# Seventeen late prefetch slots in the room of the split activations, four experts' second weights by column halves, a second result buffer and outputs in four pieces

## The chip, the cores and the metric

The kernel runs on one core of one Trainium2 chip. Times are device microseconds of that core: the median of the runs of one kernel, and for the profile the time of one profiled execution and its span from the first to the last instruction.

## What is computed

Three layers follow one another. Pooled softmax attention over 32 heads gives x (2304 tokens by 512). A feed-forward layer with an ELU replaces it. Last comes a soft mixture of eight experts: a softmax over the tokens gives each of 32 slots a weighted sum of tokens, each expert runs its four slots through two matrices, and a softmax over the slots spreads the results back over the tokens.

```
scores = scale * np.matmul(q_pool, k.transpose(0, 1, 3, 2))     # per head, 576 x 1152
attn_out = softmax(scores) @ v
h = x @ w_in;  g = np.where(h > 0.0, h, np.exp(np.minimum(h, 0.0)) - 1.0);  x = g @ w_out
logits = x @ phi                                                # 2304 x 32
slot_input = softmax(logits, 0).T @ x
for e in range(E):
    slot_out[e] = np.maximum(slot_input[e] @ w1[e], 0.0) @ w2[e]
return softmax(logits, 1) @ slot_out
```

`w1` is (8, 512, 1024) and `w2` is (8, 1024, 512), both float32: 33.5 MB together, read once. The output is 2304 x 512 float32, 4.7 MB.

## The kernel before

The whole program is first recorded as a list of operations (`add`), each with a due time, a duration, what it reads and what it writes. `Plan.run` then lays them out on the five engines by a list schedule, and the order that it finds is the order in which each engine's instructions are emitted. Space in the on-chip memory is carved by name out of a few big tiles: `memr` (split operands of TensorE), `memf` (plain float32), `memy` and `memz`. `plan.region` tells the planner which names share space, so an operation on a name waits for all users of the names that held the space before it. `swap` closes the big tiles `memy` and `memz` late in the program and opens new ones in their room, called `memyq` and `memzq`. Every DMA that the sections below speak of is issued from SyncE (SP), in order.

In the attention and feed-forward phases TensorE works on operands split into a high and a low part. The parts of the ELU's result are `H#` and `L#`, five buffers each, in `memr`. `C3T` holds the final softmax (`combine`, one call for each of the four batches, with five transposes each at L1105), `xn1` to `xn3` and `XN` the token tiles of the last slot sums (`tok_all`, L1038 to L1048).

The last phase streams the expert weights. They are cut into 64 units of 512 KB each. Units 0 to 31 are `w1` (rows of 4 KB), used by `stage1` (L1230). The others are `w2`, used by `stage2` (L1266): 24 units of kind 2 (whole rows, 2 KB) for the first six experts, and for the last `NLAST` = 2 experts eight units of kind 3, which hold one half of the columns (rows of 1 KB), first all of half m = 0, then all of half m = 1. `spare` lists the slots that hold a unit: 18 in `memyq` and `memf`, which come free during the feed-forward phase, and 11 in `memzq`, which come free when the feed-forward phase has ended. A unit whose number is past the slots goes into the slot of an earlier one, in a ring, once TensorE has read that; two of the slots are used only once. When half m is complete in `psC`, `finish(m)` (L1279 to L1304) sums it, multiplies by `C3T`, scales nine pairs of token tiles on VectorE and ScalarE into one buffer `OSB`, and writes them in pieces of `OGRP` = 6 tiles, so six output DMAs of 768 KB in all. Both halves use the same `OSB`.

Of the kernel before, what the change touches and what calls it, by code (L numbers as in the profile page):

```python
# [26 lines left out]
def act(n, psum=False):  # L27
    return n * 0.0009 + (0.135 if psum else 0.165)
# [6 lines left out]
def dve2(n):  # L35
    return n / 1920 + 0.145
# [14 lines left out]
class Plan:  # L51
# [11 lines left out]
    def add(self, t, eng, dur, fn, r=(), w=(), size=0.0, mode="F", port=False, fixed=False):  # L63
        if isinstance(eng, str):
            eng, dur = (eng,), (dur,)
        cls = (self.tag or str(self.phase)) + "".join(x.rstrip("0123456789") for x in w[0][:2] if isinstance(x, str)) + (eng[0] if len(eng) == 1 else "*")
        self.ops.append([t, len(self.ops), eng, dur, fn, r, w, size * (0.75 if self.phase == 2 else 1.0), BIAS[3 if self.tag else self.phase], t + PRI.get(cls, 0.0), cls, mode, port, fixed])

    def region(self, name, lo, hi):
        self.base[name] = (lo, hi)  # L70
# [196 lines left out]
EP = 1.3  # L267
SLOT = 14.8061
EAV = [26.8636, 30.7913, 35.1115]
OGRP = 6  # L270
DQ = [-10, 0.61]
DK = [[-9, 0.3], [-9, 0.3]]
UC = -14
# [6 lines left out]
TOKLAG = 2.0  # L280
TAIL0 = 21.9927
CMB = 2.7419
NLAST = 2


@with_exitstack
def attention_moe_softmoe(
# [12 lines left out]
    nc = tc.nc  # L300
# [207 lines left out]
    def copy_(out_, in_):  # L508
        return lambda e: nc.scalar.copy(out_, in_) if e == "ACT" else nc.vector.tensor_copy(out_, in_)  # L509
# [346 lines left out]
    def elu(n, f, t):  # L856
        A, uk, ek, hk, lk = (("A", "h", n, f), ("E", "m", n, f), ("U", "m", n, f), ("H", "m", n, f), ("L", "m", n, f))

        def ph():
            return got(psA, A)[:, :, :NH]  # L860

        add(t, "ACT", act(NQ, True), lambda: nc.scalar.activation(got(Ef, uk), ph(), AF.Relu, scale=-1.0), r=[A], w=[uk])  # L862
        add(t + 0.6, "ACT", act(NQ), lambda: nc.scalar.activation(
            got(Uf, ek), got(Ef, uk), AF.Exp, scale=-1.0), r=[uk], w=[ek])
        add(t + 1.2, "DVE", dve(NQ), lambda: nc.vector.scalar_tensor_tensor(
            got(Ef, uk), got(Uf, ek), -1.0, ph(), ALU.add, ALU.max), r=[ek, A], w=[uk])
        add(t + 2, ("ACT", "DVE"), (act(NQ), dve2(NQ)), lambda e: copy_(got(Hr, hk), got(Ef, uk))(e), r=[uk], w=[hk])
        add(t + 2.6, ("DVE", "Pool"), (dve(NQ), pool(NQ)),
            lambda e: sub_(got(Lr, lk), got(Ef, uk), r32(got(Hr, hk)))(e), r=[uk, hk], w=[lk] + ([("elu", f)] if n == NSLOT - 1 else []))

    def o_mm(n, c, t, t0):
        w, b = slots[n]
        g = w % NG
        last = n == NSLOT - 1
        x = KD * t + c
        k = x % 2 if last else t
        po_, ck = (lambda: psC[k][:, :NH]), ("C", k)
        if last and x % 4 > 1:
            ck = ("A", "o", c, t)
            po_ = lambda: got(psA, ck)[:, 0, :NH]  # L880
        d = X[b][:, c, t * NH : (t + 1) * NH]

        def mm():
            i = 0
            for f in range(GF):
                o = f * DM + c * P
                h, l = got(Hr, ("H", "m", n, f))[:, t], got(Lr, ("L", "m", n, f))[:, t]
                wh, wl = (BW["o", w % 2, x]()[:, o : o + P] for x in "hl")
                for a, x in ((wh, h), (wh, l), (wl, h)):
                    nc.tensor.matmul(po_(), lhsT=a, rhs=x, start=(i == 0), stop=(i == 3 * GF - 1))  # L890
                    i += 1
# [26 lines left out]
    def logits_split(b, t0):  # L918
        A = ("A", "lg", b)
        for c in range(KD):  # L920
            hk, lk = ("H", "lg", b, c), ("L", "lg", b, c)
            src = v3(X[b][:, c], 2)
            xr = [("X", b, c, 0), ("X", b, c, 1)]

            def mm(c=c, hk=hk, lk=lk):
                for x in (got(Hr, hk), got(Lr, lk)):
                    for t in range(2):
                        nc.tensor.matmul(got(psA, A)[: 2 * NS, t, :NH], lhsT=PH[:, c], rhs=x[:, t],
                                         start=(c == 0 and x is got(Hr, hk)), stop=(c == KD - 1 and x is got(Lr, lk)))
# [341 lines left out]
    def finish(m, t):  # L1271
# [12 lines left out]
        for x in range(0, NT, per):  # L1284
# [90 lines left out]
```

## Time and profile before

| | us |
|---|---|
| median of 3 runs | 997.66 |
| lowest and highest of the 3 | 996.82, 1002.28 |
| the profiled execution's own time | 997.68 |
| its span, first to last instruction | 995.6 |

TensorE is busy for 958.6 us of the span. The profile's page cuts the span into 40 slices of 24.9 us. The feed-forward phase ends near 905 us. What follows is the last 90 us: slot sums, expert weights and outputs.

### The profile page before, as it was taken

What the parts mean: (1) busy time and instruction counts of PE and PEld (TensorE: products, weight loads), DVE (VectorE), ACT (ScalarE), POOL (GpSimd) and SP (SyncE); (2) the same over time, 40 slices, a digit from 0 to 9 for tenths busy, and PEclk for the clock granted to TensorE, in tenths of its full rate; (3) what the DMA queues carried; (4) which work ended last, traced back from release to release, by engine and by line L of the source; (5) the groups of instructions that cost most, each with busy time, mean ns of one, the idle gap of its engine ahead of it and who ended that gap; (6) DMA issues with size and microseconds to landing.
All of it is one profiled execution on the core that took longest, in us unless ns stands there. A gap on an engine that the chain in (4) does not pass through costs nothing.

```text
span 995.6 us, 20896 instructions
## 1 busy us (share of the span) xinstructions
PE 958.6 (96%) x8474; PEld 783.5 (79%) x8474; DVE 760.4 (76%) x1281; ACT 496.9 (50%) x887; POOL 396.3 (40%) x278
## 2 busy tenths in 40 slices
PE   7999999999999999999999999999999999998965
PEld 5777767766777777766899999999999999996423
DVE  6677798888888787899998989989758887765103
ACT  2555566555666566566664444443434475442102
POOL 2878888798888888897200000000000000000000
PEclk7999999999999999999999999999999999998996
DMA  7133424223334342202362332334330132315797
GB/s 175 45 86 85 106 73 122 72 78 113 85 85 116 85 105 61 88 16 67 105 201 89 104 121 95 107 99 162 139 116 28 43 127 86 123 47 230 288 377 267
DMA packets 101583, 114.86 MB, mean 115 GB/s; under 512 B 43632, under 2 KB 70768, under 8 KB 101488
## 3 DMA queue, kind: packets, MB, share of 16 engines
q1 hardware_dynamic: 101488, 113.55, 37.3%
q8 instruction: 66, 1.08, 0.4%
q14 instruction: 29, 0.24, 0.1%
HBM read 100.27 MB, written 13.18 MB: 114 GB/s over the span
## 4 chain that ended last, share of the span: by engine, by line
PE 85%; DVE 8%; DMA 4%; ACT 1%; SPq 1%; issue 1%; DVEq 0%; ACTq 0%
PE psC L890 20%; PE psA L851 20%; PE psC L690 14%; PE psA L683 10%; PE psS L683 5%; PE psA L614 3%; PE psS L614 3%; DVE memf L623 2%; DMA memf<-in_moe_w_dram 2%; PE psC L714 1%; PE psA L598 1%; PE psA L1230 1%; DMA memzq<-in_moe_w_dram 1%; PE psA L575 1%; DVE memf L557 1%; PE psC L659 1%
## 5 line engine op out<-in xcount | busy, mean ns | idle before, releaser
L704 POOL TENSOR_TENSOR memf<-memf 128x576 f32<-128x576 f32 x241 | 360.1, 1496 | 61.4 <-ACT memf L695 35.2
L890 PE MATMUL psC<-memr,memz 128*128 128x288 f32 x1512 | 224.7, 297 | 1.2 <-DVE memf L901 0.7
L890 PEld LDWEIGHTS psC<-memr,memz 128*128 128x128 f32 x1512 | 208.1, 188 | 4.4 <-ACT memf L509 1.6
L690 PE MATMUL psC<-memf 128*64 128x288 f32 x1152 | 174.2, 419 | 0.0
L695 ACT ACTIVATE memf<-psA 128x576 f32<-128x576 f32 x206 | 132.8, 651 | 63.0 <-PE psA L614 54.8
L623 DVE TENSOR_REDUCE memf<-psA 128x2 f32<-128x384 f32 (+3 forms) x235 | 142.5, 618 | 27.6 <-PE psA L614 14.1
L1335 POOL MEMSET memf<- 128x2048 f32 x1 | 1.8, 1809 | 388.4 <-DVE memr L512 388.4
L901 DVE TENSOR_TENSOR memf<-psC,memf 128x288 f32<-128x288 f32 x220 | 100.3, 463 | 47.6 <-PE psC L890 46.0
L623 DVE TENSOR_REDUCE memf<-psS 128x4 f32<-128x768 f32 (+1 forms) x140 | 103.5, 740 | 38.3 <-PE psS L614 20.5
L690 PEld LDWEIGHTS psC<-memf 128*64 128x64 f32 x1152 | 69.8, 136 | 48.6 <-issue 9.3
L851 PE MATMUL psA<-memz 128*128 128x288 f32 x512 | 93.8, 295 | 0.0
L862 ACT ACTIVATE memf<-psA 128x576 f32<-128x576 f32 x64 | 41.8, 652 | 102.8 <-PE psA L851 102.8
L509 ACT CAST memr<-memf 128x576 fp32r<-128x576 f32 x72 | 48.2, 674 | 74.4 <-PE psC L890 35.9
L851 PEld LDWEIGHTS psA<-memz 128*128 128x128 f32 x512 | 76.6, 188 | 0.0
L683 PE MATMUL psA<-memr 64*128 64x288 f32 x816 | 72.1, 299 | 1.8 <-DVE memf L623 1.8
L695 ACT ACTIVATE memf<-psS 128x576 f32<-128x576 f32 x82 | 53.4, 651 | 40.9 <-PE psS L614 35.4
L512 DVE TENSOR_TENSOR memr<-memf,memr 128x576 fp32r<-128x576 f32 x80 | 62.8, 791 | 6.4 <-ACT memr L509 5.9
L683 PEld LDWEIGHTS psA<-memr 64*128 64x128 f32 x816 | 59.1, 185 | 8.6 <-issue 3.9
L683 PE MATMUL psA<-memy 64*128 64x288 f32 x624 | 61.5, 302 | 0.0
L851 PE MATMUL psA<-memz,memv 128*128 128x288 f32 x256 | 52.0, 296 | 0.0
L683 PEld LDWEIGHTS psA<-memy 64*128 64x128 f32 x624 | 47.7, 188 | 4.1 <-issue 3.5
L509 ACT COPY memf<-psC 128x288 f32<-128x288 f32 (+1 forms) x66 | 26.2, 397 | 49.3 <-PE psC L1266 26.7
(209 smaller groups left out, 1602.5 us busy)
## 6 DMA issues: line engine op xcount, KB each, us to landing
memf<-wscr SPq DMA_DIRECT2D x32, 512.0 KB
memf<-in_moe_w_dram SPq DMA_DIRECT2D x30, 512.0 KB
memzq<-in_moe_w_dram SPq DMA_DIRECT2D x22, 512.0 KB
memz<-in_q_dram SPq DMA_DIRECT2D x32, 288.0 KB
memz<-in_k_dram SPq DMA_DIRECT2D x32, 288.0 KB
memf<-in_v_dram SPq DMA_DIRECT2D x16, 576.0 KB
memf<-in_moe_w_in_dram SPq DMA_DIRECT2D x32, 256.0 KB
wscr<-memf SPq DMA_DIRECT2D x32, 256.0 KB
```

The source lines that it names most:

```text
L509: return lambda e: nc.scalar.copy(out_, in_) if e == "ACT" else nc.vector.tensor_copy(out_, in_)
L512: return lambda e: ENG[e].tensor_tensor(out_, a, b, ALU.subtract)
L614: nc.tensor.matmul(tile_[:m, j, lo : lo + n * MW], lhsT=qkb["qh", i][js, o : o + m], rhs=qkb["kh", i][js, g * MW : (g + n) * MW], start=Tr ...
L623: add(t, "DVE", dve(2 * n * MW), lambda: nc.vector.reduce_max(MX[i][:m, a, :, g : g + n], v4(got(psS, tok)[:m, :, lo : lo + n * MW], n), a ...
L683: nc.tensor.matmul(sp[:, j, :NH], lhsT=qkb[w, i][js, cs] if w else ONER[js], rhs=qkb[m, i][js, hs], start=(x == 0), stop=(x == 3))
L690: nc.tensor.matmul(psC[h][j * D : (j + 1) * D, :NH], lhsT=VR[i][:, j, c], rhs=e[:, j], start=(c == 0), stop=(c == NC - 1))
L695: add(t + 0.01, "ACT", act(NQ, True), lambda: nc.scalar.activation(got(EAf, E_), got(psS, S_)[:, :, :NH], AF.Exp, scale=1.0 / 16.0), r=[S_ ...
L704: ENG[e].tensor_tensor(ac, a, got(EAf, E_), ALU.add)
L851: nc.tensor.matmul(ph[:, t, :NH], lhsT=a, rhs=x, start=(i == 0), stop=(i == 3 * KD - 1))
L862: add(t, "ACT", act(NQ, True), lambda: nc.scalar.activation(got(Ef, uk), ph(), AF.Relu, scale=-1.0), r=[A], w=[uk])
L890: nc.tensor.matmul(po_(), lhsT=a, rhs=x, start=(i == 0), stop=(i == 3 * GF - 1))
L901: add(t0 + 0.8, "DVE", dve(NH), lambda: nc.vector.tensor_tensor(d, po_(), d, ALU.add), r=[ck], w=XK)
```

## The change

- `H#` and `L#` move from `memr` to the end of `memz`, which grows by their room (5,760 floats in each partition); `memr` shrinks by as much. When `memz` is swapped for `memzq`, its room holds 17 slots instead of 11, so there are 35 slots in place of 29.
- `xn1` to `xn3`, which used the room of `H#`, now lie over `C3T` and `C3`, and `SO3` over `XN`.
- `NLAST` is 4: the last four experts' `w2` goes by column halves, 16 units of kind 3 and 16 of kind 2.
- Half m = 1 has a result buffer of its own, `OS1`, in `memzq`.
- Each half is written in four pieces: 2, 4, 6 and 6 tiles for m = 0, and 6, 6, 4 and 2 for m = 1.
- The planner counts a weight's transfer at 0.67 of its size in place of 0.75.

```diff
-OGRP = 6
+OGRP = [[2, 6, 12, 18], [6, 12, 16, 18]]
-NLAST = 2
+NLAST = 4
...
-    SIZE = {"r": 15232 - 2 * KD * NQ, "f": 24456, "v": ND, "y": KD * NQ * 2, "z": 7 * ND + 2 * KD * NQ}
+    SIZE = {"r": 15232 - 2 * KD * NQ - 10 * NQ, "f": 24456, "v": ND, "y": KD * NQ * 2, "z": 7 * ND + 2 * KD * NQ + 10 * NQ}
...
-    Hr = [v3(x, 2) for x in carve("r", "H#", 5, NQ)]
-    Lr = [v3(x, 2) for x in carve("r", "L#", 5, NQ)]
+    zo = 7 * ND + 2 * KD * NQ
+    Hr = carve("z", "H#", 5, NQ, off=zo, late=True)
+    Lr = carve("z", "L#", 5, NQ, off=zo + 5 * NQ, late=True)
...
-        kind, off = ("v", 0) if i == 0 else ("r", plan.base[("H#", 0)][0] - BASE["r"] + (i - 1) * 2 * DM)
+        kind, off = ("v", 0) if i == 0 else ("r", plan.base[("C3T", 0)][0] - BASE["r"] + (i - 1) * 2 * DM)
...
-    SO3 = over("r", "SO3", 2, HM, "H#", 0, 4 * ND)
-    OSB = v3(over("f", "OSB", 1, NT * HM, "X", 2)[0], NT)
+    SO3 = over("r", "SO3", 2, HM, "XN")
+    OS0 = v3(over("f", "OS0", 1, NT * HM, "X", 2)[0], NT)
+    oz = 12 * ND
+    plan.region(("OS1", 0), BASE["z"] + oz, BASE["z"] + oz + NT * HM)
...
-    spare("z", 0, ts(32.55), 11)
+    spare("z", 0, ts(32.55), 17)
...
-            if (x + per) % OGRP == 0:
-                t0 = x + per - OGRP
-                dma(t + 2.7 + 0.3 * (x + per), out[t0 * P : (x + per) * P, m * HM : (m + 1) * HM].rearrange("(a p) c -> p a c", p=P),
-                    OSB[:, t0 : x + per], [("OSB", 0, y) for y in range(t0, x + per, per)] + [("loads", 0)], [("out", m, t0)], 512 * OGRP * HM, 0.5)
+            if x + per in OGRP[m]:
+                t0 = max([0] + [y for y in OGRP[m] if y <= x])
+                add(t + 2.7 + 0.3 * (x + per), "SP", 0.5, lambda t0=t0, t1=x + per: nc.sync.dma_start(
+                    out[t0 * P : t1 * P, m * HM : (m + 1) * HM].rearrange("(a p) c -> p a c", p=P), osb(m)[:, t0:t1]),
+                    r=[(f"OS{m}", 0, y) for y in range(t0, x + per, per)] + [("loads", 0)], w=[("out", m, t0)], size=512 * (x + per - t0) * HM)
```

Up to the last feed-forward slot the order of every engine is the same in both programs. The rows that follow are SyncE's DMAs, from the last units loaded ahead of `memzq` to the end; `in_moe_w_dram` is either expert matrix, and the last column is the tile (128x1024 is a `w1` unit, 128x2x512 a unit of kind 2, 128x4x256 one of kind 3). Before:

```order
L1215 DMA memf<-in_moe_w_dram 128x1024 x3
L515 DMA memf<-wscr 128x1024
L1215 DMA memf<-in_moe_w_dram 128x1024 x3
L1215 DMA memzq<-in_moe_w_dram 128x1024 x11
L1215 DMA memyq<-in_moe_w_dram 128x1024 x3
L1215 DMA memyq<-in_moe_w_dram 128x2x512
L1215 DMA memf<-in_moe_w_dram 128x2x512 x12
L1215 DMA memzq<-in_moe_w_dram 128x2x512 x11
L1215 DMA memyq<-in_moe_w_dram 128x4x256 x4
L1215 DMA memf<-in_moe_w_dram 128x4x256 x4
L515 DMA out_dram<-memf 128x6x256 x6
```

And of the change, from the same place:

```order
L1226 DMA memf<-in_moe_w_dram 128x1024
L1226 DMA memf<-in_moe_w_dram 128x2x512 x2
L520 DMA memf<-wscr 128x1024
L1226 DMA memf<-in_moe_w_dram 128x1024 x3
L1226 DMA memzq<-in_moe_w_dram 128x1024 x16
L1226 DMA memzq<-in_moe_w_dram 128x2x512
L1226 DMA memyq<-in_moe_w_dram 128x2x512 x4
L1226 DMA memf<-in_moe_w_dram 128x2x512 x9
L1226 DMA memf<-in_moe_w_dram 128x4x256 x3
L1226 DMA memzq<-in_moe_w_dram 128x4x256 x13
L1322 DMA out_dram<-memf 128x2x256
L1322 DMA out_dram<-memf 128x4x256
```

Behind these stand two pieces of six tiles from `memf` and four pieces of 6, 6, 4 and 2 tiles from `memzq`. From the first `memzq` row on there are 46 units in both programs: 14 of `w1`, 24 of kind 2 and 8 of kind 3 before, and 16, 14 and 16 now; 17 of them wait only for `memzq`, where 11 did.

The next rows are TensorE's between the last slot sums (L1042, L1047 now) and the first matmuls of `stage1` (L1230, L1241 now). L1105 (L1110 now) are `combine`'s transposes, L1322 (L1334 now) turns the finished slot sums. Before:

```order
L1042 MATMUL psC_80<-memr 64x512 x6
L1105 MATMUL psB_6063<-ident,memr 96x128
L1105 MATMUL psB_6064<-ident,memr 96x128
L1105 MATMUL psB_6063<-ident,memr 96x128
L1105 MATMUL psB_6064<-ident,memr 96x128
L1322 MATMUL psB_6063<-slot_sum,memf 128x32 x4
L1105 MATMUL psB_6064<-ident,memr 96x128 x2
L1105 MATMUL psB_6063<-ident,memr 96x128
L1230 MATMUL psA_78<-memyq,memf 32x512 x4
```

And of the change:

```order
L1047 MATMUL psC_80<-memr 64x512 x6
L1334 MATMUL psB_6064<-slot_sum,memf 128x32 x4
L1110 MATMUL psB_6063<-ident,memr 96x128 x2
L1110 MATMUL psB_6064<-ident,memr 96x128
L1241 MATMUL psA_78<-memyq,memf 32x512 x4
```

Seven transposes stood there and three stand there now. Before, six more stood ahead of them (four among the last feed-forward matmuls, two beside the slot sums); now the other 17 stand inside and behind `stage1`.

The last place is TensorE's end. psC_80 collects half m = 0 and psC_81 half m = 1; L1279 and L1297 (L1290 and L1308 now) are `finish`'s matmuls. Before:

```order
L1266 MATMUL psC_80<-memyq,memf 32x256 x16
L1266 MATMUL psC_81<-memf 32x256 x4
L1279 MATMUL psB_6064<-memf 96x256
L1266 MATMUL psC_81<-memf 32x256 x4
L1297 MATMUL psB_6063<-memr 128x256 x2
L1297 MATMUL psA_78<-memr 128x256 x2
L1297 MATMUL psB_6064<-memr 128x256 x2
L1297 MATMUL psA_79<-memr 128x256 x2
L1266 MATMUL psC_81<-memf 32x256 x8
```

And of the change:

```order
L1277 MATMUL psC_81<-memzq,memf 32x256 x4
L1290 MATMUL psB_6064<-memf 96x256
L1277 MATMUL psC_81<-memzq,memf 32x256 x8
L1308 MATMUL psB_6063<-memr 128x256 x2
...
L1277 MATMUL psC_81<-memzq,memf 32x256 x4
L1308 MATMUL psB_6063<-memr 128x256 x2
...
L1277 MATMUL psC_81<-memzq,memf 32x256 x16
L1290 MATMUL psB_6064<-memf 96x256
```

A unit of kind 3 is four matmuls here. The first half's `finish` now stands among eight units of half m = 1, with all its nine pairs ahead of the last four; before it stood among four, with four pairs ahead of the last two units and the other five behind them.

## Rows read from the trace of the kernel before

**Rows 1.** The profile's page: span, busy time, traffic in 40 slices.

```profile
span 995.6 us, 20896 instructions
...
PE 958.6 (96%) x8474; PEld 783.5 (79%) x8474; DVE 760.4 (76%) x1281; ACT 496.9 (50%) x887; POOL 396.3 (40%) x278
...
GB/s 175 45 86 85 106 73 122 72 78 113 85 85 116 85 105 61 88 16 67 105 201 89 104 121 95 107 99 162 139 116 28 43 127 86 123 47 230 288 377 267
```

**Rows 2.** Windows: length, engines' busy time, PEclk, DMA share, GB/s (last).

```profile
906.20:921.15 14.95, 12.62 (x53) 6.33 (x51) 7.46 (x22) 7.02 (x25) 0.00 (x0) 0.78 0.98 383
911.00:920.00 9.00, 6.81 (x29) 3.63 (x29) 3.88 (x16) 4.71 (x18) 0.00 (x0) 0.69 1.02 412
921.15:926.90 5.75, 5.18 (x41) 2.44 (x45) 1.56 (x8) 1.25 (x6) 0.00 (x0) 0.98 0.08 14
926.90:976.40 49.50, 39.23 (x385) 15.32 (x377) 2.56 (x20) 4.64 (x13) 0.00 (x0) 0.93 1.03 369
936.00:963.00 27.00, 21.95 (x223) 10.45 (x215) 2.45 (x19) 2.71 (x9) 0.00 (x0) 0.94 1.05 387
965.00:975.00 10.00, 5.52 (x57) 1.54 (x54) 0.00 (x0) 0.37 (x1) 0.00 (x0) 0.88 1.09 349
976.40:980.20 3.80, 3.80 (x33) 2.45 (x26) 1.69 (x3) 1.68 (x5) 0.00 (x0) 0.61 0.07 24
980.20:994.20 14.00, 5.68 (x30) 4.17 (x30) 6.63 (x11) 4.45 (x11) 0.00 (x0) 0.71 0.98 336
994.20:995.60 1.40, 0.00 (x0) 0.00 (x0) 0.00 (x0) 0.00 (x0) 0.00 (x0) 0.50 0.03 10
```

**Rows 3.** Timeline of SyncE's DMA issues: start, length of the group, count.

```profile
905.21 7.39 SPq L1215 DMA_DIRECT2D memzq<-in_moe_w_dram  x11
925.83 1.75 SPq L1215 DMA_DIRECT2D memyq<-in_moe_w_dram  x4
...
956.68 7.30 SPq L1215 DMA_DIRECT2D memyq<-in_moe_w_dram  x4
...
979.24 10.42 SPq L515 DMA_DIRECT2D out_dram<-memf  x6
```

**Rows 4.** The chain that ended last, in order of time: start, length.

```profile
892.62 0.22 PE psB L1105 x2
...
936.16 10.76 DMA memf<-in_moe_w_dram
...
946.98 11.00 DMA memzq<-in_moe_w_dram
```

**Rows 5.** Timeline around the start of the expert phase.

```profile
920.60 0.74 DVE L1018 SCALAR_TENSOR_TENSOR memf<-psC,memf 64x512 f32<-64x512 f32 x1 [3.87 <-PE psC L1042]
...
921.72 0.29 DVE L1084 CAST memr<-memyq 128x160 fp32r<-128x160 f32 x1
...
923.89 1.92 PE L1230 MATMUL psA<-memyq,memf 128*32 128x512 f32 x16
```

**Rows 6.** Timeline of the last units and of `finish`.

```profile
967.68 0.64 PE L1266 MATMUL psC<-memyq,memf 128*32 128x256 f32 x8 [0.45 <-DMA memyq<-in_moe_w_dram]
...
972.17 0.79 PE L1266 MATMUL psC<-memyq,memf 128*32 128x256 f32 x8 [0.85 <-DMA memyq<-in_moe_w_dram]
973.01 0.37 ACT L509 COPY memf<-psC 128x256 f32<-128x256 f32 x1 [26.29 <-PE psC L1266]
...
974.68 1.17 PE L1279 MATMUL psB<-memf 128*96 128x256 f32 x2
...
975.89 0.37 ACT L509 CAST memr<-psB 96x256 fp32r<-96x256 f32 x1 [2.50 <-PE psB L1279]
...
981.43 0.64 PE L1279 MATMUL psB<-memf 128*96 128x256 f32 x2 [0.16 <-DVE memf L1304]
...
982.11 0.42 DVE L509 CAST memr<-psB 96x256 fp32r<-96x256 f32 x1 [0.23 <-PE psB L1279]
...
987.94 1.29 DVE L1304 TENSOR_TENSOR memf<-psB,memf 128x512 f32<-128x512 f32 x2 [0.96 <-DMA out_dram<-memf]
```

More of the change, by code (lines that the diff above doesn't have):

```diff
@@ L66, in add @@
         cls = (self.tag or str(self.phase)) + "".join(x.rstrip("0123456789") for x in w[0][:2] if isinstance(x, str)) + (eng[0] if len(eng) == 1 else "*")
-        self.ops.append([t, len(self.ops), eng, dur, fn, r, w, size * (0.75 if self.phase == 2 else 1.0), BIAS[3 if self.tag else self.phase], t + PRI.get(cls, 0.0), cls, mode, port, fixed])
+        self.ops.append([t, len(self.ops), eng, dur, fn, r, w, size * (0.67 if self.phase == 2 else 1.0), BIAS[3 if self.tag else self.phase], t + PRI.get(cls, 0.0), cls, mode, port, fixed])
     def region(self, name, lo, hi):
@@ L352, in got, with hl @@
         return pool[plan.phys[key]]
+    def hl(pool, key):
+        return v3(pool[plan.phys[key]](), 2)
     def bank(tok):
@@ L438, in attention_moe_softmoe @@
     C3 = carve("r", "C3", 1, len(NT5) * 3 * NS)[0]
+    top["r"] = plan.base[("C3T", 0)][0] - BASE["r"] + 6 * DM
     XN = [v3(x, 2) for x in carve("r", "XN", 1, 2 * DM)]
@@ L866, in elu @@
             got(Ef, uk), got(Uf, ek), -1.0, ph(), ALU.add, ALU.max), r=[ek, A], w=[uk])
-        add(t + 2, ("ACT", "DVE"), (act(NQ), dve2(NQ)), lambda e: copy_(got(Hr, hk), got(Ef, uk))(e), r=[uk], w=[hk])
+        add(t + 2, ("ACT", "DVE"), (act(NQ), dve2(NQ)), lambda e: copy_(hl(Hr, hk), got(Ef, uk))(e), r=[uk], w=[hk])
         add(t + 2.6, ("DVE", "Pool"), (dve(NQ), pool(NQ)),
-            lambda e: sub_(got(Lr, lk), got(Ef, uk), r32(got(Hr, hk)))(e), r=[uk, hk], w=[lk] + ([("elu", f)] if n == NSLOT - 1 else []))
+            lambda e: sub_(hl(Lr, lk), got(Ef, uk), r32(hl(Hr, hk)))(e), r=[uk, hk], w=[lk] + ([("elu", f)] if n == NSLOT - 1 else []))
     def o_mm(n, c, t, t0):
@@ L886, in mm @@
                 o = f * DM + c * P
-                h, l = got(Hr, ("H", "m", n, f))[:, t], got(Lr, ("L", "m", n, f))[:, t]
+                h, l = hl(Hr, ("H", "m", n, f))[:, t], hl(Lr, ("L", "m", n, f))[:, t]
                 wh, wl = (BW["o", w % 2, x]()[:, o : o + P] for x in "hl")
@@ L925, in mm @@
             def mm(c=c, hk=hk, lk=lk):
-                for x in (got(Hr, hk), got(Lr, lk)):
+                for k, x in enumerate((hl(Hr, hk), hl(Lr, lk))):
                     for t in range(2):
                         nc.tensor.matmul(got(psA, A)[: 2 * NS, t, :NH], lhsT=PH[:, c], rhs=x[:, t],
-                                         start=(c == 0 and x is got(Hr, hk)), stop=(c == KD - 1 and x is got(Lr, lk)))
-            add(t0 + c, ("ACT", "DVE"), (act(NQ), dve2(NQ)), lambda e, src=src, hk=hk: copy_(got(Hr, hk), src)(e), r=xr, w=[hk])
+                                         start=(c == 0 and k == 0), stop=(c == KD - 1 and k == 1))
+            add(t0 + c, ("ACT", "DVE"), (act(NQ), dve2(NQ)), lambda e, src=src, hk=hk: copy_(hl(Hr, hk), src)(e), r=xr, w=[hk])
             add(t0 + c + 0.7, ("DVE", "Pool"), (dve(NQ), pool(NQ)),
-                lambda e, src=src, hk=hk, lk=lk: sub_(got(Lr, lk), src, r32(got(Hr, hk)))(e), r=xr + [hk], w=[lk])
+                lambda e, src=src, hk=hk, lk=lk: sub_(hl(Lr, lk), src, r32(hl(Hr, hk)))(e), r=xr + [hk], w=[lk])
             add(t0 + c + 1.5, "PE", pe(4 * NH), mm, r=[hk, lk, ("PH", 0)], w=[A])
@@ L1164, in attention_moe_softmoe, with osb @@
     SEL = over("f", "SEL", 1, 3 * NS, "E#", 0, NE * 8 * MQ + 2 * HM)[0]
-    SO3 = over("r", "SO3", 2, HM, "H#", 0, 4 * ND)
-    OSB = v3(over("f", "OSB", 1, NT * HM, "X", 2)[0], NT)
+    SO3 = over("r", "SO3", 2, HM, "XN")
+    OS0 = v3(over("f", "OS0", 1, NT * HM, "X", 2)[0], NT)
+    oz = 12 * ND
+    plan.region(("OS1", 0), BASE["z"] + oz, BASE["z"] + oz + NT * HM)
+    def osb(m):
+        return v3(MEM["z"][:, oz : oz + NT * HM], NT) if m else OS0
     SIZv = SIZ.rearrange("p (c e m) -> p c e m", c=KD, m=MQ)
@@ L1301, in scale @@
                     for k in range(per):
-                        nc.scalar.mul(OSB[:, x + k], ps2()[:, k], RC[:, x + k : x + k + 1])
+                        nc.scalar.mul(osb(m)[:, x + k], ps2()[:, k], RC[:, x + k : x + k + 1])
                 else:
-                    nc.vector.tensor_tensor(OSB[:, x : x + per], ps2(), RC[:, x : x + per].unsqueeze(2).to_broadcast([P, per, HM]), ALU.mult)
+                    nc.vector.tensor_tensor(osb(m)[:, x : x + per], ps2(), RC[:, x : x + per].unsqueeze(2).to_broadcast([P, per, HM]), ALU.mult)
             add(t + 2 + 0.3 * x, "PE", pe(per * HM), mm, r=[("SO3", m)] + [("C3T", 0, y) for y in blocks], w=[pf])
             add(t + 2.3 + 0.3 * x, ("ACT", "DVE"), (per * (act(HM, True) + 0.05), dve(per * HM)), scale,
-                r=[pf] + [("RC", *y) for y in blocks], w=[("OSB", 0, x)])
-            if (x + per) % OGRP == 0:
-                t0 = x + per - OGRP
-                dma(t + 2.7 + 0.3 * (x + per), out[t0 * P : (x + per) * P, m * HM : (m + 1) * HM].rearrange("(a p) c -> p a c", p=P),
-                    OSB[:, t0 : x + per], [("OSB", 0, y) for y in range(t0, x + per, per)] + [("loads", 0)], [("out", m, t0)], 512 * OGRP * HM, 0.5)
+                r=[pf] + [("RC", *y) for y in blocks], w=[(f"OS{m}", 0, x)])
+            if x + per in OGRP[m]:
[3 more added lines that the diff above has]
+                    r=[(f"OS{m}", 0, y) for y in range(t0, x + per, per)] + [("loads", 0)], w=[("out", m, t0)], size=512 * (x + per - t0) * HM)
     t = ts(NSLOT) + 8 + 7 + TDT[-1] * 4 + 4
```

## The prediction, made before the changed kernel ran

> **What bounds the kernel now.** I read the page first: TensorE is busy for 96% of the span, so for 900 us nothing that the change touches can pay, except through TensorE's order, which is the same up to the last feed-forward slot. The last two slices of the traffic line, 377 and 267 GB/s, are the busiest of the whole program [rows 1]; there the bound changes. So I cut the end by windows [rows 2] until each stretch had one rate. The reader is to see five stretches. From 906.2 to 921.15 the eleven units that wait for `memzq` pass. From 921.15 to 926.9 the DMA engines stand almost idle (14 GB/s). From 926.9 to 976.4 they are full with 35 units, at a rate that depends on the unit: 412 GB/s where only `w1` passes, 387 for kind 2, 349 for kind 3. From 976.4 to 980.2 they are idle again. From 980.2 to 994.2 they write the output at 336 GB/s, and 1.4 us later the program ends. In the full stretch TensorE waits for data before every unit: 0.85 us before each of the late ones, which start 1.50 us apart [rows 6]. The chain of waits agrees: it runs through DMAs that took 10.76 and 11.00 us from issue to landing [rows 4], which is eight times 1.355 us, the time of one 524 KB unit at 387 GB/s. So SyncE keeps eight units in the line, and they pass one after the other. That is a line and no sharing: the first kind 3 unit was issued at 956.68 [rows 3], and the windows still show the kind 2 rate until 963 [rows 2].
>
> So from 906 us on, the end is set by how long the DMA engines need for 46 units and 4.7 MB of output, and by the two pauses of 5.75 and 3.8 us in between.
>
> **Room in `memzq`.** Issue starts when the feed-forward phase lets go of `memz`, at 905.21 [rows 3]. `H#` and `L#` are read for the last time by the same matmuls that read the last weights in `memz`, so their move adds no wait there. What may move it is that four of `combine`'s transposes no longer stand among the last feed-forward matmuls; of these 0.22 us is in the chain that ended last [rows 4]. I take 0.2 us, so transfers begin at 906.0.
>
> The first pause exists because the slots in `memzq` were full and the first reloads had to wait until `stage1` had read a slot: 925.83, which is 1.94 us after its first matmul [rows 3, 5]. Six more units now fill the pause. By the rows: eleven units took 14.95 us with their start; five more of `w1` at 524 KB / 412 GB/s = 1.27 us make 6.4; that is 927.4. Then 14 units of kind 2 at 1.355 us (19.0), and 16 of kind 3 at 524 / 349 = 1.50 us (24.0): the last unit has passed at 970.4, where before it was 976.4. The same unit prices give the old 35 units 3 x 1.27 + 24 x 1.355 + 8 x 1.50 = 48.3 us, and they took 49.5: 1.2 us went into a slow start with few units in the line. So the 6.0 us are 5.75 of pause and 1.2 of slow start won, 0.2 won in front, and 8 x 0.15 = 1.2 us paid for eight more units in rows of 1 KB.
>
> Will the line stay full? The seventeenth unit has passed at 927.4 + 1.36 = 928.7; from issue to first bytes it takes 1.0 us (905.21 to 906.2), so the first reload must be issued by 927.7. It was issued at 925.83: 1.9 us to spare. What stands ahead of it on TensorE is lighter than before (three transposes for seven), and on VectorE one batch's casts stand behind the slot sums, which end at 921.34, as before [rows 5]; I take the same start of `stage1`, 923.9 or slightly earlier. The last `w1` unit lands at about 929; `stage1` needs it in the eighth of its steps of four units, and the first took 1.9 us, so no wait moves there. The 17 transposes behind and inside `stage1` cost TensorE time that it has: it was busy for 39.2 of the 49.5 us [rows 2], and the slots that matter are all released by `stage1`. Cost nothing; without that cover each would cost its wait for the copy out of PSUM, about 3.3 us for seven (920.6 to 923.9 [rows 5]), so 0.5 each.
>
> **Halves and outputs.** Half m = 0 is now complete eight units (12 us) before the end of the loads, and `finish(0)` with all its nine pairs stands ahead of the last four units. Its outputs are therefore issued while loads still stand in the line and pass right behind them: the second pause is gone in its first part. One half is 2.36 MB, at 336 GB/s 7.0 us: 970.4 to 977.4.
>
> Half m = 1 has to go through `finish` first. Old landings: kind 3 units started TensorE at 967.68 and every 1.50 us, so the eighth would have at 978.2, 1.8 us after the rate fell at 976.4. From there the old half m = 0 gives the steps: last matmuls to copy 0.84 us (972.17 to 973.01), copy 0.37, the sum to its cast 0.68 at the full clock (981.43 to 982.11) or 1.21 at half (974.68 to 975.89), and from that cast to the first output issue 3.35 (975.89 to 979.24) [rows 3, 6]. With hops of 0.05 that is 5.3 to 5.8; I take 5.5, in the middle, since the granted clock was at 2.4 GHz in some of these windows and at 1.2 GHz in others. The three pairs of this first piece are as many as the six tiles then. So 970.4 + 1.8 + 5.5 + 0.95 (979.24 to 980.2, issue to bytes) = 978.6. The line is empty for 1.2 us, then 7.0 us of output, then 1.4: the span ends at 987.0. The old tail was 3.8 + 14.0 + 1.4 = 19.2, the new one is 16.6.
>
> The result buffer of its own takes away a wait of 0.96 us on VectorE that ended with an output [rows 6]; it was hidden, since the output in progress kept the DMA engines at 336 GB/s. Two more DMAs than before: below by nothing, above by 0.95 + 1.4 = 2.35 us each if each had to land before the next starts. Six pieces passed in 14.0 us with no pause of that size, so nothing is the near end and I take it.
>
> The page "DMA: Bandwidth & Descriptors" of the Trainium skill speaks against cutting outputs: its section "Rules for kernel authors" wants 1 MiB or more per DMA, and its fit for one DMA (measured on GpSimd's path) is 2.0 us plus bytes / 436 GB/s. Taken one after the other, eight pieces by that would be an estimate of 26.8 us in place of 14.0. The old six would have needed 22.8 us; the trace gave them 14.0, so the fixed part overlaps here.
>
> **Sum.** Loads 6.0 us earlier, tail 2.6 us shorter: 8.6 us. The profiled execution took 997.68, with 2.08 us around its span; it stands at the median of 997.66. 997.7 - 8.6 = 989.0.
>
> **Rivals.**
> *The line runs dry after all.* `stage1` starts late, because the casts and copies of a batch queue on VectorE and ScalarE ahead of the slot transposes, or slots are not read as fast as they are asked for. Each microsecond beyond the spare 1.9 us is lost. With 2 us lost: 991.0. For it: those engines have more in front of `stage1` than before. Against: TensorE's three transposes.
> *Outputs share with loads.* If the pieces of half m = 0 took turns with the loads in the line, the last load would land up to 7.0 us later, at 979.2 instead of 972.2, and `finish(1)` would run with an empty line: 979.2 + 5.5 + 0.95 + 7.0 + 1.4 = 994.1, a time of 996.1. Against it stands the sharp step between the rates near 964.
> *Slower: `combine` ahead of `stage1`.* All four batches now wait until the last slot sums have let go of the room. If TensorE got to `stage1` only behind all 17 moved transposes (0.5 each, 8.5 us) and their casts (three of 0.29 us for each batch [rows 5], 3.5 us), it would start 12 us late, the line would be dry for 10 us, and the time 999: slower by 0.1%. It decides from a start of `stage1` at 934.4 on (923.9 + 1.9 + 8.6), and for more than 0.5% from 939.4. Against it: only three stand ahead.
> *The pieces serialise*, each paying its 2.35 us: seven pauses, 16.5 us, 1005. The old six pieces speak plainly against it. The fit for one DMA in "DMA: Bandwidth & Descriptors" of the Trainium skill would make this case.
> *The new slots bring nothing*, since `memz` is let go later by as much as the pause was worth: then only the tail's 2.6 us less 1.2, 996.3.
>
> **How the numbers follow.** The forecast 0.74, with a range of its own of 987.3 to 991 (chain of `finish(1)` between 5.3 and 5.8 and its gap closing; a `w1` rate of 400 to 430; output at 325 to 349 GB/s; half a microsecond in `memz`). Dry line 0.13, shared line 0.07, late `stage1` 0.03, serial pieces 0.01, no use of the slots 0.02. The range 986.8 to 993 holds the forecast and a dry line of up to 4 us, which leaves out about 0.13. A measurement of this kernel can tell about 0.5% from no change, here 5 us, so faster is below 992.7: the forecast and most of the dry line, 0.86. Shared line, no use and the rest of the dry one are within 0.5%: 0.11. Slower 0.03.
>
> **What would show it.** Right: no window with less than 300 GB/s between 908 and 977; 17 `memzq` issues from about 905.0, the last near 920; `stage1` at 923 to 924 and a reload within 2 us; the rate falling to 349 near 946; outputs behind the loads without a pause, and then one of about a microsecond. Wrong: a trough near 929, TensorE waiting for `combine`'s copies before `stage1`, kind 3 units landing more than 1.50 us apart once outputs are issued, or pauses between the pieces.

## The result, and the profile after

The changed kernel took 988.75 us (median of 5 runs, 988.2 to 992.23). The kernel before, beside it, took 998.56 (median of 5). The ratio is 0.9903, with a 95% interval of 0.9876 to 0.9929: faster by 1.0%. Two later series gave 0.9923 [0.9894, 0.9951] and 0.9903 [0.9882, 0.9925]. The predicted time was 989.0.

The profiled execution is the slowest of those five: 992.23 us, span 990.1. Its page, the lines of [rows 1]:

```profile
span 990.1 us, 20893 instructions
...
PE 955.2 (96%) x8474; PEld 782.5 (79%) x8474; DVE 757.0 (76%) x1278; ACT 497.7 (50%) x891; POOL 396.2 (40%) x278
...
GB/s 177 45 86 85 106 74 122 67 78 119 86 85 117 74 73 75 63 72 34 65 219 113 117 95 131 106 98 110 157 86 107 32 97 107 65 107 109 402 362 317
```

TensorE has as much to do as before. The last three slices now carry 402, 362 and 317 GB/s, where they had 288, 377 and 267 [rows 1]: the third from last held the first pause.

SyncE's issues, as in [rows 3]:

```profile
908.74 14.98 SPq L1226 DMA_DIRECT2D memzq<-in_moe_w_dram  x17
929.64 2.44 SPq L1226 DMA_DIRECT2D memyq<-in_moe_w_dram  x4
...
971.34 3.79 SPq L1322 DMA_DIRECT2D out_dram<-memf  x4
980.72 4.21 SPq L1322 DMA_DIRECT2D out_dram<-memzq  x4
```

The first `memzq` issue stands 3.53 us later than before. Ahead of it TensorE's order is the same but for four transposes of `combine` at 892 and 894 us; VectorE's differs earlier, from 807 us on, where a cast of `combine` no longer stands. Nearly all of the 3.53 us arises at a wait near 346 us, which the profile of the kernel before and one of the three profiles of the changed kernel don't have (last section). So everything below is counted from that first issue; I write it F. From F to the end of the span it was 995.6 - 905.21 = 90.4 us before, and it is 990.1 - 908.74 = 81.4 now. Two more profiled executions of the changed kernel gave 81.0 and 81.7. The saving is 8.7 to 9.4 us; the prediction's terms give 90.4 - 8.4 = 82.0, since 0.2 of its 8.6 us lie ahead of F.

The windows, to be set against [rows 2] (columns as there: length, busy times, PEclk, DMA share, GB/s):

```profile
909.70:928.70 19.00, 15.12 (x75) 7.35 (x77) 8.21 (x25) 7.29 (x25) 0.00 (x0) 0.86 1.00 392
926.35:929.65 3.30, 3.30 (x21) 1.00 (x24) 0.00 (x0) 0.42 (x2) 0.00 (x0) 0.56 1.05 415
931.00:949.00 18.00, 17.54 (x189) 7.33 (x181) 1.61 (x11) 3.23 (x9) 0.00 (x0) 1.00 1.05 386
953.00:973.00 20.00, 16.57 (x168) 8.00 (x161) 3.37 (x11) 3.89 (x14) 0.00 (x0) 0.83 1.10 348
974.00:979.80 5.80, 3.65 (x42) 1.81 (x34) 1.48 (x3) 1.38 (x5) 0.00 (x0) 1.00 1.08 380
979.80:981.60 1.80, 1.73 (x10) 1.24 (x10) 1.80 (x4) 1.80 (x6) 0.00 (x0) 0.93 0.40 143
981.60:988.60 7.00, 0.73 (x4) 0.44 (x3) 1.03 (x2) 1.13 (x3) 0.00 (x0) 0.50 1.01 337
988.60:990.10 1.50, 0.00 (x0) 0.00 (x0) 0.00 (x0) 0.00 (x0) 0.00 (x0) 0.50 0.01 1
```

The first pause (14 GB/s for 5.75 us) is gone: while `stage1` takes its first step, the line runs at 415 GB/s. That step on TensorE, to be set against the 1.92 us of [rows 5]:

```profile
926.35 3.30 PE L1241 MATMUL psA<-memyq,memf 128*32 128x512 f32 x16
```

The rates by kind of unit are the old ones: 386 for kind 2, 348 for kind 3. Behind the loads come the outputs of m = 0, and they pass at 380 GB/s, not at the 336 of before. Then there is one gap, 1.8 us at 143 GB/s, which is 1.0 us lost against 337; the outputs of m = 1 pass at that 337.

`finish(1)`, the rows that answer to [rows 6]:

```profile
974.71 0.16 PEld L1277 LDWEIGHTS psC<-memzq,memf 128*32 128x32 f32 x8 [0.32 <-DMA memzq<-in_moe_w_dram]
...
976.10 0.64 PE L1277 MATMUL psC<-memzq,memf 128*32 128x256 f32 x8 [0.74 <-DMA memzq<-in_moe_w_dram]
976.80 0.37 ACT L514 COPY memf<-psC 128x256 f32<-128x256 f32 x1 [2.37 <-PE psC L1277]
977.23 0.67 PE L1290 MATMUL psB<-memf 128*96 128x256 f32 x2 [0.49 <-ACT memf L514]
977.94 0.37 ACT L514 CAST memr<-psB 96x256 fp32r<-96x256 f32 x1 [0.76 <-PE psB L1290]
...
980.72 4.21 SPq L1322 DMA_DIRECT2D out_dram<-memzq  x4
```

From the last unit's matmuls to the first output issue it takes 4.62 us.

### The profile page after: what moved, and what is told of

Its sections match the earlier page's. It is cut to its first block, busy times and chain, and to the rows that moved or that the text cites. A ratio compares the mean times of both kernels' runs of the same rounds, so it can differ in the third digit from the quotient of the medians.

```text
span 990.1 us, 20893 instructions
## 1 busy us (share of the span) xinstructions
PE 955.2 (96%) x8474; PEld 782.5 (79%) x8474; DVE 757.0 (76%) x1278; ACT 497.7 (50%) x891; POOL 396.2 (40%) x278
## 4 chain that ended last, share of the span: by engine, by line
PE 85%; DVE 8%; DMA 3%; ACT 1%; issue 1%; SPq 0%; ACTq 0%; DVEq 0%
PE psC L895 20%; PE psA L856 20%; PE psC L695 13%; PE psA L688 10%; PE psS L688 5%; PE psA L619 3%; PE psS L619 2%; DVE memf L628 2%; DMA memzq<-in_moe_w_dram 2%; PE psA L1241 2%; PE psC L719 1%; PE psA L603 1%; DMA memf<-memf 1%; PE psA L580 1%; PE psC L664 1%; PE psC L1277 1%
## 5 line engine op out<-in xcount | busy, mean ns | idle before, releaser
L895 PE MATMUL psC<-memz 128*128 128x288 f32 x1512 | 224.6, 296 | 1.2 <-DVE memf L906 0.7
L895 PEld LDWEIGHTS psC<-memz 128*128 128x128 f32 x1512 | 208.1, 188 | 4.6 <-ACT memf L514 1.6
L906 DVE TENSOR_TENSOR memf<-psC,memf 128x288 f32<-128x288 f32 x220 | 100.3, 462 | 47.4 <-PE psC L895 45.6
L514 ACT CAST memz<-memf 128x576 fp32r<-128x576 f32 (+1 forms) x94 | 69.2, 749 | 82.6 <-PE psC L895 42.1
L517 DVE TENSOR_TENSOR memz<-memf,memz 128x576 fp32r<-128x576 f32 (+1 forms) x108 | 96.9, 906 | 9.8 <-ACT memz L514 8.6
L870 DVE SCALAR_TENSOR_TENSOR memf<-memf,psA 128x576 f32<-128x576 f32 x64 | 47.6, 744 | 1.7 <-ACT memf L868 1.6
```

Of the source, the lines that this page charges most:

```text
L517: return lambda e: ENG[e].tensor_tensor(out_, a, b, ALU.subtract)
```

## Experiments

**Which half of the change pays.** Two kernels each keep one part: the first all but the new slots, the second the slots with the old tail. A third has half of the new slots.

```diff
-    spare("z", 0, ts(32.55), 17)
+    spare("z", 0, ts(32.55), 11)
```

That is the edit of the first; the third puts 14 there. The second keeps the 17 and instead sets `NLAST = 2`, six tiles in every piece, and gives both halves the buffer `OS0`.

> The changed kernel with 11 slots in memzq in place of 17, all else as in the change. Measured from the first memzq issue to the end of the span, the kernel before took 90.4 us and the change 81.4. Full line (the six more slots fill the pause): the pause of 5 to 6 us is back, the last unit has passed 72.4 us after that issue (71.2 as before and 1.2 for eight more units in 1 KB rows), the tail stays at the change's 16.1, so 88.5 us and a time of about 996. Rival, order (the gain comes from combine's transposes having moved, or from stage1 starting earlier): 81 to 83 us, about 989 to 990. Rival, tail (the gain comes mainly from the halves and pieces at the end): about 84 to 85 us, 991 to 992.

> The changed kernel with 17 slots, but the end as before: two experts by column halves, one result buffer for both halves, pieces of six tiles. Full line: the last unit passes 64.1 us after the first memzq issue (65.3 in the change less 8 x 0.15), and the old tail of 19.2 us comes back, so 83.3 us and a time of about 990.6. Rival, tail: most of the gain is gone, 88 us or more, 995 to 997. Rival, order: 81 to 83 us.

> The changed kernel with 14 slots in memzq. Full line: three of the six units are missing, 14 units have passed 19.8 us after the first issue, the first reload's bytes come at 21.9 as before, so the line is dry for 2 us and then slow for up to a microsecond: 83.5 to 84.5 us, a time of 991 to 992, about half way between 11 and 17 slots. Rival, order: 81 to 82 us. Rival with a threshold (any pause at all costs the whole): 88 us.

Measured: 11 slots 998.71 us (ratio 0.9987 [0.9969, 1.0005]), from F to the end 90.8 us. Slots with the old tail 993.4 (0.9941 [0.9922, 0.9961]), 84.0 us. 14 slots 994.92 (0.9951 [0.9934, 0.9969]), 85.6 us.

With 11 slots the rest of the change (the tail, the moved buffers, `combine`'s new place) comes to no difference that can be measured. The timeline of SyncE, and `stage1`'s first step on TensorE, in that kernel:

```profile
907.46 6.66 SPq L1226 DMA_DIRECT2D memzq<-in_moe_w_dram  x11
930.41 1.75 SPq L1226 DMA_DIRECT2D memyq<-in_moe_w_dram  x4
...
926.76 3.64 PE L1241 MATMUL psA<-memyq,memf 128*32 128x512 f32 x16
```

And its windows around the pause:

```profile
908.50:922.50 14.00, 11.30 (x48) 5.48 (x46) 6.08 (x17) 6.53 (x21) 0.00 (x0) 0.83 0.99 397
923.00:931.80 8.80, 7.92 (x39) 3.45 (x43) 1.86 (x8) 0.74 (x3) 0.00 (x0) 0.52 0.03 8
```

The pause is back in its old place and is 8.8 us long, 3.05 longer than before [rows 2]: `stage1` starts at F + 19.3 (before, 923.89 - 905.21 = 18.7), and its first step takes 3.64 us where it took 1.92 [rows 5], at a granted clock of 0.52, nearly the level of 1.2 GHz. The expected 88.5 us left that out. The longer step is not peculiar to 11 slots: in all eleven profiles with the change's order and nothing put ahead of `stage1`, it takes 2.97 to 3.64 us; why the clock is low there was not tried. The new tail is there all the same, as that kernel's windows at the end of its loads show:

```profile
965.00:981.00 16.00, 12.99 (x96) 4.64 (x97) 1.97 (x4) 2.31 (x6) 0.00 (x0) 0.57 1.10 349
982.00:988.00 6.00, 3.82 (x43) 1.93 (x42) 1.65 (x4) 1.56 (x5) 0.00 (x0) 1.00 1.04 364
```

The loads end about 981.8, and from there it is 16.5 us to the end of the span (998.3), where the old tail took 19.2. So the longer pause eats what the tail saves: with the tail's gain below, 90.4 + 3.05 - 2.3 to 3.0 = 90.4 to 91.1, and 90.8 was measured.

With 14 slots the first reload is issued at F + 21.7, and the line is low for 3.5 us, as a window shows:

```profile
928.00:931.50 3.50, 3.50 (x24) 0.88 (x20) 0.00 (x0) 0.00 (x0) 0.00 (x0) 0.51 0.28 114
```

Half of the gain is thus left by half of the slots. The 85.6 us are 1.1 above the expected 83.5 to 84.5: 0.8 is the reload, which was expected at the F + 20.9 of the change; the rest was not looked for. The slots with the old tail have no first pause (381 GB/s over 63 us) and the old second one, in the windows of that kernel:

```profile
907.50:970.50 63.00, 53.62 (x470) 23.43 (x468) 12.22 (x50) 13.45 (x47) 0.00 (x0) 0.91 1.04 381
970.50:974.70 4.20, 4.20 (x37) 2.16 (x37) 2.12 (x4) 1.58 (x4) 0.00 (x0) 0.76 0.12 40
974.80:988.80 14.00, 5.92 (x27) 4.28 (x26) 6.36 (x11) 4.37 (x11) 0.00 (x0) 0.66 0.96 327
```

From F on the slots alone are thus worth 90.4 - 84.0 = 6.4 us. Against 81.0 to 81.7 for the whole change, the new tail is worth another 2.3 to 3.0.

**Is the spare time before the line runs dry what the profile said?** TensorE is held up ahead of `stage1` by matmuls of no use, 12 in one kernel and 40 in another; the output doesn't depend on them.

```diff
+    def idle():
+        for i in range(12):
+            nc.tensor.matmul(psC[1][:NS, :256], lhsT=ident[:, :NS], rhs=SIZ[:, 256 * (i % 4) : 256 * (i % 4 + 1)], start=True, stop=True)
+
+    add(t + 1.4, "PE", 12 * 0.107, idle, r=[("SIZ", 0)], w=[("C", 1)])
```

> The changed kernel with twelve matmuls of no use on TensorE ahead of stage1, which starts later by 1.3 us (at 2.4 GHz) to 2.6 us (at 1.2 GHz). Full line: the first reload may be issued 1.6 us later than it was in the change's trace without a pause in the line, so 0 to 1 us more than 81.4. Rival, stage1 sets the end: the whole 1.3 to 2.6 us more.

> The same with forty such matmuls: stage1 starts later by some D between 4.3 and 8.5 us, to be read from its trace. Full line: the line runs dry for D less 1.6 us (3 to 7), with a dip in the traffic between the memzq loads and the first reload, and the end is later by as much. Rival, stage1 sets the end: later by the whole of D. Rival, the reloads were not what the line waited for: no dip and no more than 1 us.

The matmuls cost several times what I had set: 7.5 us for the 12 and 19.9 for the 40. TensorE's rows, the first two with 12 and the last with 40:

```profile
924.05 7.54 PE L1353 MATMUL psC<-memf,ident 128*32 128x256 f32 x24
...
931.88 1.93 PE L1241 MATMUL psA<-memyq,memf 128*32 128x512 f32 x16
...
926.64 19.86 PE L1353 MATMUL psC<-memf,ident 128*32 128x256 f32 x80
```

So the delays are read from SyncE's timeline. With 12:

```profile
905.52 15.58 SPq L1226 DMA_DIRECT2D memzq<-in_moe_w_dram  x17
933.82 1.92 SPq L1226 DMA_DIRECT2D memyq<-in_moe_w_dram  x4
```

A window between these two rows, of the same kernel:

```profile
928.80:934.60 5.80, 5.80 (x43) 2.31 (x45) 0.00 (x0) 0.43 (x2) 0.00 (x0) 1.00 0.08 30
```

With 40:

```profile
908.21 15.07 SPq L1226 DMA_DIRECT2D memzq<-in_moe_w_dram  x17
948.72 2.93 SPq L1226 DMA_DIRECT2D memyq<-in_moe_w_dram  x4
```

The first reload moved from F + 20.9 to F + 28.3 (7.4 later) and F + 40.5 (19.6 later). From F to the end it took 87.6 and 100.3 us, 6.2 and 18.9 more than the 81.4 of the changed kernel. The times were 995.09 (0.997 [0.9947, 0.9992]) and 1005.91 us (1.0069 [1.0045, 1.0093]). The line runs dry about F + 23.3, where 17 units have passed, and from there a delay is paid in full, less 0.7 to 1.2 us. The spare time itself is 1.4 us (F + 23.3, less the 1.0 from issue to first bytes, less F + 20.9); the 0.2 to 0.7 us in between would be a slow restart of the line, which was not measured by itself. So the end hangs on this one wait. A straight line between the two ratios crosses 1 at a reload 11 us later than in the changed kernel; the third rival had put its point of decision at 10.5.

**Pieces and buffers.** The two sizes of pieces that are new are taken back (six tiles throughout), and in another kernel the second buffer.

```diff
-OGRP = [[2, 6, 12, 18], [6, 12, 16, 18]]
+OGRP = [[6, 12, 18], [6, 12, 18]]
```

```diff
-        return v3(MEM["z"][:, oz : oz + NT * HM], NT) if m else OS0
+        return OS0
```

> The changed kernel with the outputs in three pieces of six tiles for each half. Full line: the pieces of the first half stand in line behind the loads in any size, and the first piece of the second half has six tiles either way, so 81.4 us, within half a microsecond, and about 989. Rival, small pieces pay (a short last piece lands sooner): 1 to 2 us more. Rival, each DMA costs something fixed: up to 2 us less. In the trace the first half's pieces should pass at the 383 GB/s that the change shows if it is standing in line that makes them fast, and at 337 if it was the size of the pieces.

> The changed kernel with one result buffer for both halves. Full line: the pieces of the first half have landed by the time their tiles are written again, but for the last six tiles, which land about 981.6 in the change's trace where the seventh pair is due at 981.2; so at most 0.5 us more than the change's 81.4 us from the first memzq issue, and the time stays near 989. Rival, the buffer is what shortens the tail: 2 to 3 us more, about 991.5.

> The changed kernel once more, beside the others of this group: 81.4 us from the first memzq issue to the end, within half a microsecond. The time that lies ahead of that issue should be nearer to the 905.2 of the kernel before than to 908.7, since the order of the program is the same up to there; if it is 908.7 again, the move of the split activations costs 3.5 us in the earlier phases, which the prediction left out.

From F to the end: 81.0 us with six tiles, 81.2 with one buffer, 81.0 for the changed kernel once more. Times 990.82, 988.78 and 991.16; ratios 0.9914 [0.9889, 0.994], 0.9912 [0.9884, 0.994] and 0.9923. Both edits are worth nothing within the 0.7 us by which three profiles of one kernel differ. With six tiles the outputs of m = 0 pass as fast, as its windows show (second line: those of m = 1):

```profile
972.50:978.00 5.50, 3.35 (x40) 1.45 (x29) 1.04 (x3) 0.97 (x3) 0.00 (x0) 1.00 1.08 379
980.20:986.80 6.60, 0.65 (x4) 0.36 (x2) 0.87 (x2) 0.94 (x3) 0.00 (x0) 0.50 1.01 342
```

So it isn't the size of the pieces that makes them fast.

**Can the tail be shortened further?** One kernel has three experts by halves; one has three and a small first piece for m = 1; the changed kernel ran beside them, and then four experts with the small first piece.

```diff
-NLAST = 4
+NLAST = 3
...
-OGRP = [[2, 6, 12, 18], [6, 12, 16, 18]]
+OGRP = [[2, 6, 12, 18], [2, 6, 12, 18]]
```

> Edit: three experts by column halves in place of four, so 18 units of kind 2 and 12 of kind 3; nothing else. Read by the time from the first memzq issue to the end of the program, which was 81.0 to 81.4 us with four. Theory (the line of transfers sets the end): four units pass at the 2 KB rate in place of the 1 KB rate, 4 x 0.14 = 0.6 us less, and half m = 0 is complete 9 us before the last load in place of 12, its chain of some 5 us still fits ahead: 80.4 to 80.8. Rival (half m = 0 becomes late, so that its outputs no longer stand in the line behind loads and pass at 340 GB/s with a pause in front): 82 or more. In the median this is under what the measurement can tell.

> Edit: three experts by column halves, and half m = 1 written in pieces of 2, 4, 6 and 6 tiles, so that its first output waits for one pair of tiles in place of three. Read by the time from the first memzq issue to the end. Theory (the gap of 1.5 us between the outputs of the two halves is the chain of finish(1)): two pairs fewer are ahead of the first output, 0.7 to 1.0 us, so the gap closes to 0.5 to 0.8: 79.6 to 80.1. Rival (a small DMA into an empty line does not fill it, so the rate builds up as late as before): no better than three halves alone, 80.4 to 80.8.

> The changed kernel itself, beside the two others on the same chip: from the first memzq issue to the end 81.0 to 81.4 us by every theory; ratio to the kernel before 0.990 to 0.992.

> Edit: four experts by column halves as in the changed kernel, half m = 1 written in pieces of 2, 4, 6 and 6 tiles. Read by the time from the first memzq issue to the end, 81.0 to 81.7 in the changed kernel's three profiles. Theory (the gap behind the outputs of m = 0 is the chain of finish(1), and with four experts the outputs of m = 0 stand in the line behind loads): no pause ahead of the outputs of m = 0, these at 380 GB/s, and the first issue of m = 1 3.3 us behind the copy of its sum, as with three experts and the same pieces, in place of 3.9 to 4.3; the gap of 1.5 us shrinks to 0.5 to 0.9, and the time to 80.2 to 80.8. Rival (four small steps gain nothing, as with three experts): 81.0 to 81.7 again.

From F to the end: 81.3, 81.5, 81.7 and 80.85 us. Times 992.83 (0.9922 [0.9897, 0.9947]), 989.65 (0.9902 [0.988, 0.9924]), 990.14 (0.9903) and 990.26 (0.9917 [0.9898, 0.9936]).

Both theories on three halves fail on the number: neither 80.4 to 80.8 nor 82. The rival's mechanism is there, at a smaller price. Windows of three experts by halves:

```profile
967.00:973.00 6.00, 5.57 (x39) 1.81 (x40) 0.49 (x2) 0.74 (x2) 0.00 (x0) 0.57 1.09 348
973.00:975.00 2.00, 2.00 (x21) 1.46 (x20) 1.58 (x3) 1.69 (x5) 0.00 (x0) 1.00 0.68 224
975.00:988.00 13.00, 5.54 (x41) 3.43 (x39) 5.22 (x9) 5.33 (x14) 0.00 (x0) 0.92 0.98 336
```

The line drops just when the loads have passed, since the outputs of m = 0 were issued at 973.65, after the last bytes, and they then pass at 336 GB/s throughout. I had counted the head start of 9 us against the last landing; the line is empty some 2 us before that, and an issue needs another microsecond to bytes. What the faster units saved went there. Four experts give a head start just long enough: 971.34 against the end of the loads between 973 and 974.

The small first piece with three halves fails on the number too (81.5, not 79.6 to 80.1). Its pause between the halves is gone, but the pause ahead of the outputs of m = 0 stands, and the end doesn't move:

```profile
970.80:972.80 2.00, 2.00 (x21) 1.46 (x20) 1.47 (x3) 1.57 (x4) 0.00 (x0) 1.00 0.48 163
973.00:986.40 13.40, 5.53 (x41) 3.41 (x39) 5.21 (x9) 5.30 (x14) 0.00 (x0) 0.90 1.00 341
```

The small first piece does what was expected of it when four experts go by halves. The timeline of that kernel, and below it its windows over the outputs of m = 0 and the gap:

```profile
974.95 0.37 ACT L514 COPY memf<-psC 128x256 f32<-128x256 f32 x1 [2.72 <-PE psC L1277]
...
978.22 3.63 SPq L1322 DMA_DIRECT2D out_dram<-memzq  x4
```

```profile
972.00:977.00 5.00, 2.67 (x35) 0.73 (x23) 0.82 (x2) 0.97 (x3) 0.00 (x0) 1.00 1.09 384
977.80:979.20 1.40, 1.32 (x9) 1.04 (x8) 1.40 (x3) 1.40 (x4) 0.00 (x0) 0.87 0.46 162
```

The first issue comes 3.27 us behind the copy, in place of 980.72 - 976.80 = 3.92. The end, 80.85, is the lowest of all kernels, but only 0.2 to 0.9 below the three profiles of the changed kernel, and the medians can't tell them apart. It is not shown to be better.

## Why the prediction was right

**The bound.** The end is set by the line of transfers and its pauses: every kernel above moves by what its pauses say, from 80.85 to 100.3 us.

**Slots, 6.0 us.** Expected were the last load at 970.4 - 905.0 = F + 65.4 and the rates 412, 387 and 349. The rates measured were 386 and 348 for the last two; the first stretch of 19.0 us moved 392 x 19.0 = 7.45 MB, the 14.2 units that its prices give; and the loads ended between 973 and 974, F + 64.3 to 65.3. The third rival's wait ahead of `stage1` and the shared line are both refuted: the reload came at F + 20.9, and once outputs had been issued at 971.34 the last two units still followed each other by no more than the line's step of 1.50 us (974.71 and 976.10, 1.39 apart).

**The spare 1.9 us** was right by luck in part. `stage1` did start earlier, at F + 17.6 in place of 18.7. That the three transposes in place of seven are the reason is likely and not shown: with 11 slots and the same three it started at F + 19.3. But its first step took 3.30 us where the prediction put 1.9, at a granted clock of 0.56 in that window (nearly the level of 1.2 GHz; of the 19.0 us up to 928.70 TensorE had been busy for 15.1). With 12 matmuls of no use ahead TensorE had worked without a break since 924.05, the granted clock was 1.00, the level of 2.4 GHz, and the first step took 1.93 us. What sets the clock there was not tested by itself. The earlier start and the longer step nearly cancel. The rival of the dry line was nearer than its 0.13 says: the reload of another profile of the changed kernel came at F + 21.7, 0.6 us ahead of the F + 22.3 by which it had to be issued.

**Tail, 2.6 us.** By the prediction it should have been worth 2.6 - 1.2 = 1.4 us net of the 1 KB rows; it was 2.3 to 3.0. The changed kernel's tail, from the end of the loads (about 973.8) to 990.1, took 16.3 us where the prediction has 16.6. The term that was mis-sized is the chain of `finish(1)`: 4.62 us in place of 5.5, all at the full clock, and 5.05 in another profile. The last landing took half of that back, 2.3 us behind the end of the loads in place of 1.8. The larger part of the difference lies on the other side of the comparison: in the kernel with the slots alone the old tail took 20.0 us (970.5 to 990.5) in place of the 19.2 of [rows 2], with a pause of 4.2 us and outputs at 327 GB/s. By these, 20.0 - 16.3 - 1.2 = 2.5. The output rate of m = 0 was wrong too: I took 336 GB/s from outputs that began on an idle line, and behind loads they passed at 380, 6.2 us in place of 7.0. But that moves nothing here: the outputs of m = 1 begin only behind `finish(1)`, at 981.6, and at 336 GB/s those of m = 0 would have been through by then as well (973.8 + 7.0 = 980.8). The loss of 1.0 us in the gap agrees with the forecast 1.2 by luck: faster outputs and the late landing widen it, the shorter chain narrows it.

**Pieces and buffer, nothing.** Shown by their own experiments. The page "DMA: Bandwidth & Descriptors" of the Trainium skill asks for 1 MiB or more in one DMA for the most bandwidth ("Rules for kernel authors"); in this line pieces of 0.25 to 0.75 MiB pass as fast as pieces of 0.75 MiB (380 against 379 GB/s), so the rule doesn't bind here.

## What to carry to other kernels

When the transfers are the bound, look for the pauses in their line before anything else, and ask for each which issue was late and how long the line could have lived without it; room for a few more prefetches that cover the pause was worth the whole pause here, and half of that room about half. Read also what the change's new order does to the wait: here the longer first step made the pause of the kernel with 11 slots longer by as much as its tail saved. Give results a head start, so that they are issued before the last loads have passed, and count it against the end of the traffic and not against the last landing.

## What the runs showed of the hardware that was not expected

**Outputs behind loads pass faster than outputs alone.** In the changed kernel 380 GB/s against 337, with six tiles 379 against 342, with the small first piece 384 for m = 0. With 11 slots, where they were also issued ahead of the end of the loads, it was 364. Where the line had run empty first (three halves, the old tail) all of them pass at 327 to 341. Why is not settled; the first piece's size is not it.

**The front of the program scatters by 4.9 us.** F was between 904.19 and 909.08 in the profiles of the changed kernel and its variants, in which TensorE's order ahead of F is one and the same. Most of it is one place in the attention phase. VectorE waits there for a DMA of 2.2 KB, and TensorE for VectorE. The timeline of the changed kernel's profile with F = 908.74, a window behind the wait, and the row of the kernel before:

```profile
345.42 0.54 DVE L744 RECIPROCAL memf<-memf 18x64 f32<-18x64 f32 x1 [2.41 <-DMA memf<-memf]
...
346.43 1.32 PE L688 MATMUL psA<-memr 64*128 64x288 f32 x8 [1.68 <-DVE memf L628]
```

```profile
346.40:350.00 3.60, 3.57 (x26) 2.95 (x28) 2.00 (x4) 1.30 (x2) 1.21 (x1) 0.53 0.15 53
```

```profile
343.40 0.54 DVE L739 RECIPROCAL memf<-memf 18x64 f32<-18x64 f32 x1 [0.47 <-DMA memf<-memf]
```

After its wait of 1.68 us TensorE ran for these 3.6 us at a granted clock of 0.53, nearly the level of 1.2 GHz. Counted against the kernel before, its 3,400th matmul (near 343 us) is 0.1 us late and its 4,000th (near 403 us) 3.6. The same row and window in the profile of the changed kernel once more, with F = 904.19, show neither:

```profile
341.86 0.54 DVE L744 RECIPROCAL memf<-memf 18x64 f32<-18x64 f32 x1 [0.20 <-issue]
```

```profile
346.40:350.00 3.60, 3.60 (x48) 2.73 (x44) 3.60 (x5) 2.17 (x4) 1.59 (x2) 1.00 0.12 47
```

The third profile of the changed kernel has the wait again:

```profile
345.14 0.54 DVE L744 RECIPROCAL memf<-memf 18x64 f32<-18x64 f32 x1 [2.34 <-DMA memf<-memf]
```

So it is no single accident. In ten of the 13 profiles of the changed kernel and its variants TensorE waits there for more than 1 us (with 14 slots 1.88, F = 909.08). In four of the ten the clock fell behind the wait, and in these F is 908.58 to 909.08; in the other nine profiles it is 904.19 to 908.21. The wait alone doesn't decide on the clock: with the same wait of 1.60 us it fell in the third profile (F = 908.58) and not in the kernel with 12 matmuls (905.52). What makes the small DMA late was not tried, and the kernel before has only one profile, so whether the change brings the wait is open. The times don't show it: in the three series the medians before and after differ by 9.8, 7.3 and 9.5 us, and from F to the end the profiles differ by 8.7 to 9.4. The scatter of F is larger than the whole of the tail's gain, which is why small effects had to be read from F on.
